# When the gate is normalized: six of its eight iterations in the first half expert, two in the second, and the second matrices' preparation in the blocks between

## The chip, the core and the metric

The kernel runs on one core of a Trainium2 chip. The core has five engines with a queue each, in program order: TensorE (PE, matrix products), VectorE (DVE), ScalarE (ACT), GpSimd (POOL) and SyncE (SP, which here issues the DMAs). An instruction waits on semaphores for results of other engines; whatever stands behind it in its queue waits with it. The metric is the device time of one execution in microseconds; lower is better.

## The reference

Three stages, all in float32. An attention over 2 x 8 heads of 576 positions with a position bias; a layer of three products and a maximum (512 to 768 to 512); and a mixture of 8 experts over 1152 tokens, in which this change lies:

```
logits = x @ w_gate;  P = exp(logits - logits.max())
for _ in range(8):
    P /= P.sum(1, keepdims=True) + 1e-09      # per token: "rows"
    P /= P.sum(0, keepdims=True) + 1e-09      # per expert: "cols"
    P *= N / E
for e in range(E):
    out += P[:, e:e + 1] * (np.maximum(x @ w1[e], 0.0) @ w2[e])
```

P is 1152 x 8. The eight iterations are one chain: each needs the one before it whole.

## The kernel before

Float32 products are made of three float16 products, of a high and a low part of each operand (`h` and `l` at a name's end), scaled by powers of two that are read off the largest magnitudes.

The mixture runs as 32 blocks and 16 half experts. Block n, `up(n)`, makes a quarter of an expert's hidden layer for all tokens by Strassen's scheme: seven products of 12 matmuls each (L1229) into three PSUM banks x, z, y, in the order x, z, y, x, y, x, z. The first, third, fourth and sixth product are copied out by ACT as snapshots s1, s5, s2, s3 (L1237); the second, fifth and seventh are joined to a snapshot by DVE (L1241), and the sum of s3 and s5 is made at L1281. A bank may be started anew only when its reader has read it: the fifth product (y) waits for snapshot s5, the next block's first product (x) for s3, the next block's second product (z) for the seventh's join. ACT then makes relu's high part (L1245), DVE its low part (L1250). After the segments of a block, 0 to 6, `then` runs what is scheduled there.

Half expert h, `down(h)`, multiplies the hidden layers of blocks 2h and 2h + 1 by 512 rows of w2, in nine parts t = 0 to 8 of 12 matmuls with 512 columns (L1309), into two PSUM banks in turn; ACT (h = 0, L1314) or DVE (L1320, L1325) adds a part to `acc`. The order is block 0, 1, 2, half expert 0, block 3, 4, half expert 1, block 5, 6, and so on.

Work for what comes later is put into these by hand, as lists by segment (`between`, `extra`) or part (`todo`), and by `sched` into the sixteen steps of the layer before:

- `prep_f(n)`: the weights of block n; six steps: scaling on ACT (L948), four differences and sums on DVE (L952 to L957), high parts on ACT (L960, L964), low parts as differences on POOL (L961, L967).
- `prep_2(i)`, in lists `p2(i)`: a fourth of half expert i // 4's matrix: two ACT instructions (L1040, L1041), a difference on POOL (L1042), and a read of a later matrix on SP.
- `pk(h, kind, i)`: a largest magnitude of a weight tile, on DVE (L810); `peak_join` reduces them (L836), `peak_send` and `peak_get` pass them through DRAM to all partitions, `peak_all` reduces what landed (L807) and makes the powers of two (L783 to L853).
- `rows()`: four DVE instructions on P (L1158 to L1161). `cols(bank)`: a product with ones on PE (`pc`, L1165; the column sum), then four DVE instructions (L1166 to L1169). In `bank` ps_u it takes the z bank, in ps_d one of the two of the half experts.
- `x_steps(1)`, in lists `end(name)`: sums of the blocks' input (t1, t2, tb, t4, DVE L982), their high parts (h2 to h6, ACT L976) and low parts (l2 to l6, L972, DVE or POOL). `m_top` (L1181) and `m_spread` (L1186) bring the largest input to all partitions.

Before, the iterations are spread thus: rows in part 0 of half expert 0, cols and rows in its parts 2, 4, 6, 8, in block 3's segment 4 and block 4's segments 1 and 5, and the last cols in part 2 of half expert 1.

## Time and profile before

| | us |
|---|---|
| median of 3 runs | 1091.41 (1090.27 to 1092.1) |
| profiled execution, time | 1092.23 |
| its span, first to last instruction | 1090.4 |
| PE busy | 1047.3 |
| DVE busy | 800.1 |
| ACT busy | 589.0 |
| POOL busy | 408.4 |

The profile is one execution. An instruction's row has its start and duration from the span's start; idle time in front of it stands in brackets, with what ended it. Instructions overlap a little at their ends, so the next one can start before a row's end. The stretch that the change touches runs from about 364 us (the last steps of the layer before) to 481 us (the end of half expert 1); blocks 5 to 31 and the other half experts keep their order.

### The profile page before, as it was taken

To read this page: it belongs to the slowest core of one execution; us is meant where nothing else is said; L and a number is where in the kernel's file an instruction comes from. 1 tells how busy PE (TensorE), PEld (TensorE's weight loads), DVE (VectorE), ACT (ScalarE), POOL (GpSimd) and SP (SyncE) were. 2 spreads that over 40 slices of the span, in tenths; PEclk is the share of its full clock that TensorE was granted. 3 is DMA by queue.
4 is the path that set the end of the run, shared out by engine and by line. 5 is a ranking of instruction groups with operands and counts; after the bars stand their busy time and mean duration, and the time that the engine had idled before them with its cause. 6 is when DMAs were issued, how large, how long until landed. Compare 5 with 4: busy or idle time off the path is not lost.

```text
span 1090.4 us, 18491 instructions
## 1 busy us (share of the span) xinstructions
PE 1047.3 (96%) x7163; PEld 734.1 (67%) x7163; DVE 800.1 (73%) x1560; ACT 589.0 (54%) x1003; POOL 408.4 (37%) x285
## 2 busy tenths in 40 slices
PE   6779999999999999999999999999999999999998
PEld 3259988999899765655756657566466575665753
DVE  7999999778786878767677566676776666767633
ACT  7989988534334675444544536445445364454530
POOL 6996998122222424053231312412223124132220
PEclk8999999999999999999999999999999999999999
DMA  5888764233324013020221212302212113010002
GB/s 185 270 238 262 238 186 122 69 102 114 95 61 156 20 42 83 20 63 22 62 63 40 63 35 52 81 20 64 60 43 64 35 50 76 26 44 6 1 1 87
DMA packets 40757, 90.48 MB, mean 83 GB/s; under 512 B 8095, under 2 KB 11102, under 8 KB 39774
## 3 DMA queue, kind: packets, MB, share of 16 engines
q1 hardware_dynamic: 40526, 89.01, 28.1%
q8 instruction: 56, 0.92, 0.4%
q10 hardware_dynamic: 144, 0.29, 0.1%
q14 instruction: 31, 0.25, 0.1%
HBM read 75.20 MB, written 13.30 MB: 81 GB/s over the span
## 4 chain that ended last, share of the span: by engine, by line
PE 68%; DVE 19%; ACT 5%; DMA 4%; issue 3%; POOL 2%; DVEq 0%; SPq 0%; ACTq 0%; POOLq 0%
PE d L1309 29%; PE x L1229 11%; PE y L1229 8%; PE z L1229 7%; PE sc L479 2%; PE pv L617 2%; PE o L1080 2%; PE pt L565 2%; DVE ww L115 1%; DVE ww L120 1%; DVE ww L118 1%; POOL s L353 1%; DVE ng L496 1%; PE p L378 1%; DMA all<-peaks 1%
## 5 line engine op out<-in xcount | busy, mean ns | idle before, releaser
L1309 PE MATMUL d<-w2h,hh 128*128 128x512 f16 x576 | 218.3, 379 | 1.8 <-DVE acc L1320 1.6
L1309 PE MATMUL d<-w2h,hl 128*128 128x512 f16 x576 | 218.3, 379 | 0.2 <-DVE hl L1250 0.2
L1309 PE MATMUL d<-w2l,hh 128*128 128x512 f16 x576 | 218.3, 379 | 0.0
L1229 PEld LDWEIGHTS <-w1h 128*128 128x128 f16 x1792 | 175.5, 98 | 53.1 <-issue 5.7
L1309 PEld LDWEIGHTS <-hh 128*128 128x128 f16 x1152 | 112.6, 98 | 134.6 <-issue 3.4
L961 POOL TENSOR_TENSOR w1l<-wf,w1h 128x768 f16<-128x768 f32 x32 | 55.7, 1741 | 304.8 <-ACT w1h L960 271.4
L1245 ACT ACTIVATE hh<-s 128x576 f16<-128x576 f32 x128 | 87.3, 683 | 129.5 <-DVE s L1241 102.5
L1250 DVE SCALAR_TENSOR_TENSOR hl<-s,hh 128x576 f16<-128x576 f32 x128 | 112.6, 881 | 48.1 <-ACT hh L1245 45.6
L1325 DVE SCALAR_TENSOR_TENSOR acc<-d,kh,acc 128x512 f32<-128x512 f32 x126 | 94.0, 746 | 67.0 <-PE d L1309 65.4
L1042 POOL TENSOR_TENSOR w2l<-w2r,w2h 128x512 f16<-128x512 f32 x64 | 77.4, 1221 | 120.1 <-ACT w2h L1041 120.1
L1229 PEld LDWEIGHTS <-w1l 128*128 128x128 f16 x896 | 87.9, 98 | 23.0 <-issue 0.6
L1309 PEld LDWEIGHTS <-hl 128*128 128x128 f16 x576 | 56.4, 98 | 68.5 <-DVE hl L1250 0.7
L967 POOL TENSOR_TENSOR w1l<-wf,w1h 128x1024 f16<-128x1024 f32 x32 | 69.3, 2164 | 76.1 <-ACT w1h L964 76.1
L948 ACT ACTIVATE wf<-wr,pw 128x1024 f32<-128x1024 f32 x32 | 36.5, 1141 | 96.9 <-DVE pm L783 89.3
L1237 ACT ACTIVATE s<-x,cx 128x576 f32<-128x576 f32 x96 | 70.2, 732 | 27.5 <-PE x L1229 27.2
L1241 DVE SCALAR_TENSOR_TENSOR s<-z,cx,s 128x576 f32<-128x576 f32 x64 | 52.3, 818 | 42.7 <-ACT s L1237 31.1
L1229 PE MATMUL x<-xth,w1h 128*128 128x288 f16 x384 | 78.7, 287 | 0.7 <-ACT s L1237 0.7
L1229 PE MATMUL x<-xtl,w1h 128*128 128x288 f16 x384 | 78.8, 287 | 0.4 <-DVE xtl L972 0.4
L964 ACT ACTIVATE w1h<-wf 128x1024 f16<-128x1024 f32 x32 | 33.6, 1049 | 83.2 <-DVE wf L957 83.1
L1229 PE MATMUL x<-xth,w1l 128*128 128x288 f16 x384 | 78.4, 286 | 0.0
L668 PE MATMUL m<-xh,wl 128*128 128x384 f32 x216 | 73.5, 340 | 2.6 <-POOL wl L123 2.6
L668 PE MATMUL m<-xh,wh 128*128 128x384 f32 x216 | 73.7, 341 | 2.0 <-DVE t L899 1.9
(229 smaller groups left out, 2364.3 us busy)
## 6 DMA issues: line engine op xcount, KB each, us to landing
wr<-in_moe_w SPq DMA_DIRECT2D x50, 512.0 KB, 3.7
w2r<-in_moe_w SPq DMA_DIRECT2D x64, 256.0 KB, 2.6
bias_f<-bo SPq DMA_DIRECT2D x36, 295.5 KB, 3.5
bias<-bias_f SPq DMA_DIRECT2D x32, 288.0 KB, 2.9
qk<-in_qk SPq DMA_DIRECT2D x7, 1152.0 KB, 7.2
wr<-in_moe_w_out SPq DMA_DIRECT2D x6, 512.0 KB, 3.5
vr<-in_v SPq DMA_DIRECT2D x8, 320.0 KB, 5.8
bias<-bias_f SPq DMA_DIRECT2D x16, 144.0 KB, 4.8
```

The lines of the kernel that those rows point to most:

```text
L668: T.matmul(out=p[:, :TG], lhsT=ws[:, 128 * c:128 * c + 128], rhs=xs[:, c, TG * g:TG * g + TG], start=(c == 0 and n == 0), stop=(c == 3 and ...
L948: A.activation(out=t[:, 0:4], in_=w1r.pop(n), func=AF.Identity, scale=w_pow[n // 2, 1][:, 2:3])
L961: G.tensor_tensor(out=lo[:, 0:3], in0=t[:, 1:4], in1=hi[:, 0:3], op=ALU.subtract)
L967: G.tensor_tensor(out=lo[:, 3:7], in0=t[:, 4:8], in1=hi[:, 3:7], op=ALU.subtract)
L1042: G.tensor_tensor(out=lo, in0=r, in1=hi, op=ALU.subtract)
L1229: T.matmul(out=ps[bank][:, s, :SH], lhsT=ws[:, i, c, :], rhs=xs[:, j, c, s * SH:s * SH + SH], start=(start and k == 0), stop=(k == 5), **kw)
L1237: A.activation(out=t, in_=src, func=AF.Identity, scale=c)
L1241: V.scalar_tensor_tensor(out=out, in0=z, scalar=scale, in1=out, op0=ALU.mult, op1=ALU.add)
L1245: A.activation(out=o, in_=src, func=AF.Relu)
L1250: V.scalar_tensor_tensor(out=l, in0=src, scalar=0.0, in1=o, op0=ALU.max, op1=ALU.subtract)
L1309: T.matmul(out=pd, lhsT=hs[:, fh, 128 * t:128 * t + 128], rhs=ws, start=(k == 0), stop=(k == 11))
L1325: V.scalar_tensor_tensor(out=acc[:, t, :], in0=pd, scalar=kh[:, 1 + t:2 + t], in1=acc[:, t, :], op0=ALU.mult, op1=ALU.add)
```

## The change

No instruction is added or taken away; the order changes on every engine.

- Normalization: cols and rows now stand in parts 1, 2, 4, 5, 7 and 8 of half expert 0 (after the rows of part 0), in part 3 of half expert 1, and the last cols in its part 6. Blocks 3 and 4 have none.
- Half expert 0 keeps of its other work only the weights of blocks 3 and 4, in other parts than before. Preparation of half expert 1's matrix (p2(4) to p2(7)) goes to segments 1 and 4 of blocks 3 and 4; the maxima of expert 1's second matrix for half expert 2 (pk(2, 2, i)) to block 3's segments 3 to 6, their exchange to block 4. The maxima of the first one, pk(2, 1, i), go to steps 13 and 14 of the layer before, with a wider exchange.
- p2(1) goes from step 14 into block 0's segment 5; the sum tb and its parts h5 and l5 from step 15 into block 0.

```diff
--- before.py
+++ after.py
@@ -871,7 +871,8 @@
                         load_f(n)
                     S10 = ("a",), [(0, 1)]
                     SB = ("b",), [(1, 1), (0, 2)]
-                    SC = ("c",), [(1, 2)]
+                    SC = ("c",), [(1, 2), (2, 1)]
+                    SD = ("d",), [(2, 2)]
                     jk.append(acc.rearrange("p t d -> p (t d)")[:, 0:1024])
 
                     def size_w(i):
@@ -1067,8 +1068,8 @@
                          6: [bs0[0], pk(0, 2, 2), pk(0, 2, 3), lambda: peak_join(*SB)], 7: [b_top, bs0[1], pf1[0]],
                          8: [b_all] + xs_("t1", "tb", "h2", "l2"), 9: xs_("h3", "h5", "t2") + pf1[1:3], 10: xs_("l3", "l5", "h4") + pf1[3:4],
                          11: xs_("l4", "t4") + pf1[4:6] + [pk(1, 2, 0)], 12: xs_("h6", "g6") + [bs1[0], pk(1, 2, 1), pk(1, 2, 2)],
-                         13: [bs1[1], p2(0), pk(1, 2, 3), lambda: peak_join(*SC)], 14: [p2(1), lambda: peak_send(SC[0])],
-                         15: [lambda: last.update(x_steps(1))] + [end(n) for n in ("t1", "t2", "tb", "h3", "h4", "h5", "h2", "l2")]}
+                         13: [bs1[1], p2(0), pk(1, 2, 3), pk(2, 1, 0)], 14: [pk(2, 1, 1), lambda: peak_join(*SC)],
+                         15: [lambda: last.update(x_steps(1))] + [end(n) for n in ("t1", "t2", "h3", "h4", "h2", "l2")]}
                 evs = []
                 for n, g in enumerate((0, 2, 1, 3)):
                     for d in range(4):
@@ -1190,8 +1191,8 @@
                     V.tensor_scalar(out=nc_, in0=c, scalar1=-1.0, scalar2=None, op0=ALU.mult)
                     V.tensor_scalar(out=kx, in0=cx[:, 1:2], scalar1=xs[:, 1:2], scalar2=2.0 ** 8, op0=ALU.mult, op1=ALU.mult)
 
-                between = {(0, 0): [m_top, end("l3")], (0, 1): [m_spread, end("l4"), end("l5")], (0, 2): [end("t4")],
-                           (0, 3): [end("h6"), end("l6")], (0, 6): [p2(2)], (1, 5): [p2(3)],
+                between = {(0, 0): [m_top, end("l3")], (0, 1): [m_spread, end("l4"), end("tb")], (0, 2): [end("h5"), end("t4"), end("l5")],
+                           (0, 3): [end("h6"), end("l6")], (0, 4): [lambda: peak_send(SC[0])], (0, 5): [p2(1)], (0, 6): [p2(2)], (1, 5): [p2(3)],
                            (1, 6): [logits], (2, 1): [flip], (2, 2): [gate], (1, 2): [lambda: peak_get(SC[0])],
                            (2, 0): [lambda: peak_all(*SC)], (2, 6): []}
                 kh_t = {}
@@ -1299,6 +1300,9 @@
                             2: [fa[2], pk(h + 2, 2, 2), pk(h + 2, 2, 3), lambda: peak_join(*S2), lambda: peak_send(S2[0])],
                             3: [fa[3], lambda: peak_get(S2[0])], 4: [fa[4], fa[5]], 5: [p2(0), lambda: peak_all(*S2)],
                             6: [fb[0], fb[1], p2(1)], 7: [fb[2], fb[3], p2(2)], 8: [p2(3), fb[4], fb[5]]}
+                    if h == 0:
+                        todo = {0: [fa[0]], 1: [fa[1], fa[2]], 2: [fa[3]], 3: [fa[4], fa[5]], 4: [], 5: [fb[0]], 6: [fb[1], fb[2]],
+                                7: [fb[3]], 8: [fb[4], fb[5]]}
                     for t in range(NTT):
                         pd = ps_d.tile([128, 512], F32, tag="d", name="d")
                         k = 0
@@ -1312,15 +1316,17 @@
                         if h == 0:
 
                             A.activation(out=acc[:, t, :], in_=pd, func=AF.Identity, scale=kh[:, 0:1])
-                            if t in (2, 4, 6, 8):
+                            if t in (1, 2, 4, 5, 7, 8):
                                 cols(ps_u)
-                            if t in (0, 2, 4, 6, 8):
+                            if t in (0, 1, 2, 4, 5, 7, 8):
                                 rows()
                         elif h == 1:
                             V.scalar_tensor_tensor(out=acc[:, t, :], in0=pd, scalar=kh[:, 0:1], in1=acc[:, t, :],
                                                    op0=ALU.mult, op1=ALU.add)
-                            if t == 2:
+                            if t in (3, 6):
                                 cols(ps_u)
+                            if t == 3:
+                                rows()
                         else:
                             V.scalar_tensor_tensor(out=acc[:, t, :], in0=pd, scalar=kh[:, 1 + t:2 + t], in1=acc[:, t, :],
                                                    op0=ALU.mult, op1=ALU.add)
@@ -1334,8 +1340,11 @@
                         extra = {}
                         if n == 1:
                             extra = {i: [f] for i, f in enumerate(prep_f(2))}
-                        for seg in {3: (4,), 4: (1, 5)}.get(n, ()):
-                            extra.setdefault(seg, []).extend((lambda: cols(ps_d), rows))
+                        if n == 3:
+                            extra = {1: [p2(4)], 3: [pk(2, 2, 0)], 4: [pk(2, 2, 1), p2(5)],
+                                     5: [pk(2, 2, 2)], 6: [pk(2, 2, 3), lambda: peak_join(*SD), lambda: peak_send(SD[0])]}
+                        if n == 4:
+                            extra = {1: [p2(6)], 2: [lambda: peak_get(SD[0])], 4: [p2(7)], 6: [lambda: peak_all(*SD)]}
                         if n == 5:
                             for t in range(NTT):
                                 extra.setdefault(t % 7, []).append(
```

The first place is ACT's queue around block 3. The names are those above; `s<-x` is a snapshot of bank x. Before, from the last weights of block 4 on:

```order
L964 ACTIVATE w1h<-wf 128x1024
L1237 ACTIVATE s_5941<-x,cx 128x576
L1245 ACTIVATE hh<-s_5941 128x576
L1237 ACTIVATE s_5971<-y,cx 128x576
L1237 ACTIVATE s_5986<-x,cx 128x576
L1245 ACTIVATE hh<-s_5986 128x576
L1237 ACTIVATE s_6024<-x,cx 128x576
```

And now (lines are numbered by the changed kernel, one or four higher):

```order
L965 ACTIVATE w1h<-wf 128x1024
L1238 ACTIVATE s_5916<-x,cx 128x576
L1246 ACTIVATE hh<-s_5916 128x576
L1041 ACTIVATE w2r<-w2r,pw 128x512
L1042 ACTIVATE w2h<-w2r 128x512
L1238 ACTIVATE s_5953<-y,cx 128x576
L1238 ACTIVATE s_5968<-x,cx 128x576
L1246 ACTIVATE hh<-s_5968 128x576
L1041 ACTIVATE w2r<-w2r,pw 128x512
L1042 ACTIVATE w2h<-w2r 128x512
L1238 ACTIVATE s_6005<-x,cx 128x576
```

A pair of preparation 4 now stands in front of snapshot s5, one of preparation 5 in front of s3; block 4 has the same two places.

The second place is DVE's queue in block 3, from the fifth product's join to the seventh's. Before, with a normalization:

```order
L1241 SCALAR_TENSOR_TENSOR s_5986<-y,cx,s_5986 128x576
L1166 TENSOR_REDUCE col<-pc 128x8
L1167 TENSOR_SCALAR col<-col 128x8
L1168 RECIPROCAL col<-col 128x8
L1169 SCALAR_TENSOR_TENSOR P<-P,col 128x72
L1158 TENSOR_REDUCE row<-P 128x9
L1159 TENSOR_SCALAR row<-row 128x9
L1160 RECIPROCAL row<-row 128x9
L1161 TENSOR_TENSOR P<-P,row 128x72
L1250 SCALAR_TENSOR_TENSOR hl<-s_5986,hh 128x576
L1281 TENSOR_TENSOR s_5971<-s_6024,s_5971 128x576
L1241 SCALAR_TENSOR_TENSOR s_6024<-z,cx,s_6024 128x576
```

And now, with maxima:

```order
L1242 SCALAR_TENSOR_TENSOR s_5968<-y,cx,s_5968 128x576
L810 TENSOR_REDUCE pk<-w2r 128x1
L1251 SCALAR_TENSOR_TENSOR hl<-s_5968,hh 128x576
L1282 TENSOR_TENSOR s_5953<-s_6005,s_5953 128x576
L810 TENSOR_REDUCE pk<-w2r 128x1
L1242 SCALAR_TENSOR_TENSOR s_6005<-z,cx,s_6005 128x576
```

The normalization's eight instructions are gone from here; a maximum now stands between the sum of two snapshots and the seventh product's join.

The third place is DVE's queue where the layer before ends and block 0 begins; `xm` is a largest magnitude of the input, `t` a sum of it, `nm` the reduction that `m_top`'s transpose feeds. Before:

```order
L810 TENSOR_REDUCE pk<-w2r 128x1
L836 TENSOR_REDUCE pj<-pk 128x1
L810 TENSOR_REDUCE xm<-acc 128x1 x2
L1094 TENSOR_REDUCE m_3624<-xm 128x1
L982 TENSOR_TENSOR t<-acc 128x576
L982 TENSOR_TENSOR t<-acc,t 128x576
L982 TENSOR_TENSOR t<-acc 128x576
L1182 TENSOR_REDUCE nm_5241<-pmx 1x1
```

And now:

```order
L810 TENSOR_REDUCE pk<-w2r 128x1
L810 TENSOR_REDUCE pk<-wr_4839 128x1
L810 TENSOR_REDUCE xm<-acc 128x1
L810 TENSOR_REDUCE pk<-wr_4973 128x1
L836 TENSOR_REDUCE pj<-pk 128x1 x2
L810 TENSOR_REDUCE xm<-acc 128x1
L1095 TENSOR_REDUCE m_3624<-xm 128x1
L983 TENSOR_TENSOR t<-acc 128x576
L983 TENSOR_TENSOR t<-acc,t 128x576
L1183 TENSOR_REDUCE nm_5234<-pmx 1x1
```

Two maxima over 1024 columns moved in front of the last two `xm`; the third `t` moved behind `nm`.

## Rows read from the trace of the kernel before

**Rows 1.** Page, part 1: busy us, share of the span, instructions, by engine.
```profile
PE 1047.3 (96%) x7163; PEld 734.1 (67%) x7163; DVE 800.1 (73%) x1560; ACT 589.0 (54%) x1003; POOL 408.4 (37%) x285
```

**Rows 2.** Windows: length; busy (x) of PE, PEld, DVE, ACT, POOL; clock; DMA.
```profile
405.25:429.27 24.02, 24.02 (x117) 11.66 (x117) 19.05 (x56) 14.11 (x21) 6.12 (x4) 1.00 0.22 55
429.27:444.65 15.38, 12.45 (x88) 9.33 (x88) 11.37 (x23) 8.02 (x13) 6.46 (x5) 0.89 0.20 61
444.65:455.41 10.76, 10.76 (x91) 8.61 (x89) 8.36 (x19) 5.50 (x8) 0.00 (x0) 1.00 0.01 2
455.41:480.80 25.39, 23.83 (x113) 10.83 (x111) 19.41 (x49) 9.19 (x12) 6.07 (x4) 1.00 0.22 52
438.50:442.20 3.70, 3.70 (x18) 2.59 (x18) 0.95 (x3) 0.57 (x2) 0.00 (x0) 0.54 0.00 0
```

**Rows 3.** Timeline of PE: start, us, line, tile; idle time before and releaser.
```profile
418.39 0.34 PE L1165 MATMUL pc<-P,ones 128*128 128x72 f32 x2
...
431.71 0.28 PE L1229 MATMUL z<-xth,w1h 128*128 128x288 f16 x1 [0.81 <-DVE col L1166]
...
438.40 0.28 PE L1229 MATMUL y<-xth,w1h 128*128 128x288 f16 x1 [2.12 <-ACT s L1237]
...
478.19 0.38 PE L1309 MATMUL d<-w2h,hh 128*128 128x512 f16 x1 [0.77 <-DVE acc L1320]
```

**Rows 4.** Timeline of DVE: normalization, last difference of block 3, preparation, landed maxima.
```profile
418.76 0.23 DVE L1166 TENSOR_REDUCE col<-pc 128x8 f32<-128x72 f32 x1 [1.24 <-PE pc L1165]
...
420.48 2.03 DVE L1161 TENSOR_TENSOR P<-P,row 128x72 f32<-128x72 f32 x1
...
444.50 0.75 DVE L1281 TENSOR_TENSOR s<-s,s 128x576 f32<-128x576 f32 x1
445.37 0.82 DVE L1241 SCALAR_TENSOR_TENSOR s<-z,cx,s 128x576 f32<-128x576 f32 x1
...
468.50 0.28 DVE L836 TENSOR_REDUCE pj<-pk 128x1 f32<-128x2 f32 x2
...
476.05 0.42 DVE L807 TENSOR_REDUCE pm<-all 128x2 f32<-128x256 f32 x1 [3.03 <-DMA all<-peaks]
```

**Rows 5.** Timeline of POOL in the first half expert.
```profile
417.55 1.64 POOL L961 TENSOR_TENSOR w1l<-wf,w1h 128x768 f16<-128x768 f32 x1 [20.74 <-issue]
420.30 2.12 POOL L967 TENSOR_TENSOR w1l<-wf,w1h 128x1024 f16<-128x1024 f32 x1 [1.11 <-ACT w1h L964]
```

**Rows 6.** Timeline of ACT in the first half expert.
```profile
416.00 0.69 ACT L1314 ACTIVATE acc<-d,kh 128x512 f32<-128x512 f32 x1 [2.08 <-PE d L1309]
...
418.59 0.69 ACT L1314 ACTIVATE acc<-d,kh 128x512 f32<-128x512 f32 x1 [1.17 <-PE d L1309]
```

**Rows 7.** Timeline of ACT in block 1.
```profile
384.45 1.14 ACT L948 ACTIVATE wf<-wr,pw 128x1024 f32<-128x1024 f32 x1
...
391.60 0.71 ACT L1040 ACTIVATE w2r<-w2r,pw 128x512 f32<-128x512 f32 x1
392.35 0.63 ACT L1041 ACTIVATE w2h<-w2r 128x512 f16<-128x512 f32 x1
```

**Rows 8.** Timeline of PE in block 1: the fifth product.
```profile
386.84 0.41 PE L1229 MATMUL y<-xth,w1h 128*128 128x288 f16 x2 [0.29 <-ACT s L1237]
```

**Rows 9.** Timeline of DVE, then of PE, in block 0.
```profile
369.96 0.75 DVE L982 TENSOR_TENSOR t<-acc 128x576 f32<-128x576 f32 x1
...
370.95 0.38 PE L1186 MATMUL pmx<-nm,ones 1*128 1x1 f32 x2 [1.06 <-DVE nm L1182]
```

**Rows 10.** Chain that ended last, block 4: start, us, what.
```profile
447.87 0.17 PE pc L1165 x2
...
449.52 1.47 PE x L1229 x12
```

**Rows 11.** Groups of DVE, 405 to 481 us: busy, mean ns of one, idle.
```profile
L810 DVE TENSOR_REDUCE pk<-w2r 128x1 f32<-128x512 f32 x8 | 5.1, 677 | 0.0
L810 DVE TENSOR_REDUCE pk<-wr 128x1 f32<-128x1024 f32 x4 | 4.7, 1208 | 0.0
```

## The prediction

> **What bounds the kernel now.** I read the page's busy times first, then the chain of waits, then windows over the blocks that the change touches, then each engine's timeline there. TensorE (PE) is busy 96% of the span [rows 1], and the chain runs through it, so a move counts only where PE has to wait, or stops waiting. Both kernels issue the same products and the same other instructions; only their order differs. So the whole question is which PE stalls go and which come.
>
> The windows [rows 2] show them. The first half expert takes 24.02 us and PE is busy all through. Block 4 takes 10.76 with PE never idle, column sums included. Block 3, with the same seven products, takes 15.38. A column sum costs PE 0.17, a product 1.47 [rows 10]; block 3 has one sum where block 4 has two, so it should take 10.59 and loses 4.8. The second half expert takes 25.39; by the first, with three sums fewer, it should take 23.5: it loses 1.9. That is 6.7 us in all, the most that any order of this stretch can win.
>
> What PE waited for is in rows 3: VectorE (DVE) still held the column sum's bank (0.81); the fifth product of block 3 waited 2.12 for a snapshot of ScalarE (ACT) that stood behind a join that stood behind the normalization on DVE; and the last part of the second half expert waited 0.77 for an accumulation that stood behind the landed maxima. After the 2.12 the granted clock is 0.54 over 3.70 us, with PE busy all the time: 3.70 x 0.46 = 1.7 us of the 4.8 belong to that.
>
> [...]
>
> **The change part by part.** Times below count from the start of the half expert or product named.
>
> *The first half expert.* One part lasts (24.02 - 4 x 0.17) / 9 = 2.59. A normalization starts when the sum has landed, and its last instruction starts 1.72 later (418.76 to 420.48 [rows 4]) and takes 0.23 like the reduction before it; with 0.37 from the sum's issue to its landing (418.39 to 418.76 [rows 3, 4]) the next sum is possible 2.3 after the last. Sums in neighbouring parts are 2.59 + 0.17 = 2.76 apart, so bare normalizations fit, with 0.46 to spare. What doesn't fit is GpSimd (POOL). In row 420.48 the 72-column multiplication takes 2.03 instead of 0.23: it ends with POOL's difference of 420.30, 2.12 long [rows 4, 5]. So I let DVE instructions with two operands in SBUF wait for a POOL difference that runs. [...]
>
> The two differences start 1.55 and 1.71 after the accumulation of their part [rows 5, 6]. Part 7 (parts are counted from 0) issues the first difference of block 4's weights. Its accumulation comes 0.20 after the part's end (418.59 against 418.39), so the difference runs from 1.75 to 3.39; the sum of part 7 is issued at 0, so the last multiplication would start at 0.37 + 1.72 = 2.09, is held until 3.4, ends at 3.65, and the sum of part 8, wanted at 2.76, waits 0.9. The same sum for part 3's difference (1.91 to 4.03) against part 4's sum holds one of its instructions for 0.4 to 0.85, against 0.46 to spare: 0 to 0.45, I take 0.2. The wait of 0.81 [rows 3] goes, since nothing but the normalization is then before the bank's reading. Bounds of these two: 0 to 1.4; taken 1.1.
>
> *Block 3, fifth product.* After the sum of part 8 the normalization meets the last difference of block 4's preparation (2.12) in the same way: it ends some 1.0 later than the join could start. That is what is left of the long wait. New in front of the fifth product is preparation 4: ACT does two instructions, 391.60 to 392.98 together, 1.28 until the next can start [rows 7], between the relu and the snapshot that the fifth product needs. Block 1 shows such a case: one instruction of 1.14 (row 384.45) in the same place, and the fifth product waited 0.29, start to start 0.45 [rows 7, 8]; 1.28 instead of 1.04 (the pitch of that one) makes it 0.7. I take 0.75 for such a pair. The fifth product so waits 1.0 + 0.75 = 1.75 where it waited 2.12 (2.29 start to start) and then ran at half clock. Bounds: 0.7 (no lateness of the join) to 2.3.
>
> *Blocks 3 and 4, the other preparations.* Preparation 5 stands before the snapshot of the sixth product, on which block 4's first product waits: 0.75. The late snapshot also feeds the sum of two snapshots (row 444.50), which has two operands in SBUF like 420.48 and meets preparation 5's difference on POOL: that starts with the snapshot, lasts about 1.1 (512 of the 768 columns of 417.55, an estimate) and so holds the sum some 0.35 past the snapshot (about 0.7, as 391.60). Then come a maximum of 0.68 that stands there now [rows 11] and the join (row 445.37) that frees the bank: 0.35 + 0.75 + 0.68 + 0.82 = 2.6 after the snapshot, with which block 4's first product started; its second is wanted 1.47 later: 1.1 (0.8 if POOL doesn't hold it). In block 4 two relus, two differences, a maximum and a join follow on DVE, by the same durations about 0.35 later than the product: with preparation 6 in front of the fifth product's snapshot 0.75 + 0.35 = 1.1. Preparation 7's snapshot holds no bank that the half expert wants, but delays DVE. Together 2.95, none of it there before. Lower bound 0, if ACT (busy 5.50 of the 10.76 of block 4 [rows 2]) takes the pairs in its gaps; upper 3.9.
>
> *Second half expert.* Block 4's DVE work ends late and the maxima of expert 1's second matrices are unpacked there (about 0.75): the first accumulation ends 0.55 after the third part wants its bank, and two maxima of 1.21 behind it [rows 11] cost the fourth part another 0.35. The landing of the next maxima comes 7.55 after the last local reduction, and the last part starts 2.14 after that [rows 3, 4]; that reduction comes some 2 us after where it stood in the half expert, but the parts themselves are 0.9 and two sums later: 0.85 instead of 0.93. The accumulation that stood behind maxima and a normalization (part 5) is clear, since the normalization now follows it. Together 1.75 instead of 1.9; bounds 0.8 to 3.0.
>
> *Before the first half expert.* The wait of 1.06 before row 370.95 goes almost whole: the difference of row 369.96 (0.67 until the next) no longer stands before it, nor does one preparation's POOL work [rows 9]. That is -1.1. In front of the last maximum over the input stand two maxima of 1.21 [rows 11], mostly in DVE's idle time: +0.2; preparation 1 in block 0: +0.1. The peaks that block 2 unpacks are two instead of one, four small instructions and a wider reduction, some 0.6 (476.05 to 478.19 holds two items and an accumulation); they stand before a join on which a snapshot and with it the fifth product of block 2 hang: +0.6, or 0 if there is room. Net -0.2; bounds -1.3 to +0.8.
>
> The exchange of maxima over DRAM of the four moved ones has block 4 to land: no cost. The queue on SP gets one read of 64 KB and one of 128 KB where it had them the other way round; nothing waits there.
>
> Sum: 1.1 + 1.75 + 2.95 + 1.75 = 7.55 us of stalls instead of 6.7, and -0.2 before: +0.65. The profiled execution took 1092.23 (span 1090.4, 1.8 around it) and would take 1092.9; the median 1091.41 lies 0.8 lower, so the forecast for the median is 1092.1. All lower bounds together would give 1.5 - 6.7 - 1.3 = -6.5, all upper ones 10.6 - 6.7 + 0.8 = +4.7; the terms hang on two causes (ACT's pairs, POOL's differences), so the rivals below take them by cause.
>
> **Rivals.** (A) ACT takes the moved pairs in its gaps: then the 2.95 and 0.75 of block 3 go, +0.65 - 3.7 = -3.05, 1088.4. For it speaks that ACT is idle for half of block 4, and the pair of 391.60, after which PE doesn't wait; against it, that this pair stands behind the last snapshot of its block while the four moved ones stand in front of one, and [rows 7, 8].
>
> (B) Half clock comes again. The new stalls stand close together: 1.75, 0.75 and 1.1 within some 9 us, and 1.1 again behind them. If the clock falls once more for the 3.70 of rows 2, that costs 1.7: +2.35, 1093.8; twice, 1095.5. It decides from the point where block 3's wait reaches about the 2.12 that did it before. Against it: no single new one is as long, and the two shorter ones of the second half expert (0.77 the last) left its window at 1.00 [rows 2, 3]. [...]
>
> (C) POOL's differences and the normalizations miss each other: 1.1, the 1.0 of block 3 and 0.3 of block 4 go, +0.65 - 2.4 = -1.75, 1089.7. For it: the meeting in part 7 is decided by 0.3 us. Against it: row 420.48 met with less.
>
> **How the numbers follow.** Forecast 0.48, A 0.14, B 0.24, C 0.14. This kernel can tell about 0.2%, 2.2 us, from no change. Faster than 1089.2: A, 0.14. Slower than 1093.6: B, 0.24 (its first case is just beyond, its second well). Same: the forecast and C, 0.62. The range reaches into A and over both cases of B: 1088.9 to 1095.4; the forecast's own is 1090.4 to 1093.4.
>
> **What would show it.** Windows, each up to the next one's first product: block 3 7 x 1.47 + 1.75 + 0.75 = 12.8 instead of 15.38, block 4 10.3 + 1.1 + 1.1 = 12.5 instead of 10.76; the fifth products of both waiting on a snapshot, block 4's second product on a join; a sum of part 8 waiting about 0.9 with the multiplication before it over 1 us long; the row of 370.95 without its wait; the clock 1.00 in all of these windows. I am wrong if block 4 stays below 11.5 (then A), or if the clock is low in blocks 3 and 4 (then B).

## The result and the profile after

The changed kernel takes 1096.47 us (median of six runs, 1095.65 to 1097.51), the kernel before 1090.84 beside it (six runs, 1089.91 to 1092.19): ratio 1.0051, 95% interval 1.0038 to 1.0064. That is slower, outside the range of 1088.9 to 1095.4. Timed once more beside the kernel before (below) the ratio was 1.0042 [1.0028, 1.0056].

The profiled execution took 1095.99 (span 1094.2) against 1092.23. The windows of the changed stretch, first product to first product, in the order first half expert, block 3, block 4, second half expert (start:end, length, then busy time and count of PE, PEld, DVE, ACT, POOL, the clock, DMA):

```profile
406.58:432.30 25.72, 24.84 (x122) 11.99 (x121) 17.31 (x56) 12.55 (x18) 5.40 (x3) 1.00 0.14 41
432.30:444.94 12.64, 10.61 (x86) 8.20 (x86) 7.83 (x15) 7.21 (x11) 3.88 (x3) 1.00 0.08 22
444.94:457.56 12.62, 10.61 (x84) 8.19 (x84) 8.09 (x13) 6.96 (x11) 1.72 (x2) 1.00 0.42 30
457.56:484.57 27.01, 24.14 (x114) 11.06 (x112) 22.66 (x54) 10.49 (x15) 7.76 (x6) 1.00 0.27 72
```

Against [rows 2] block 3 gains 2.7, and everything beside it loses: 1.7, 1.9 and 1.6. The half clock is gone: the granted clock is 1.00 in all four windows, where block 3 had 0.89. Together 77.99 where it was 75.55. The path from block 0 to the first half expert loses as well: from the transposition of the input's maximum (pmx) to that half expert's first product 37.96 us instead of 37.09.

These are PE's waits in the timeline after that are new or longer than before (start, us, line, tile, idle time before and what ended it); they answer to [rows 3], the first one to [rows 9]:

```profile
370.29 0.38 PE L1187 MATMUL pmx<-nm,ones 1*128 1x1 f32 x2
...
376.87 0.41 PE L1230 MATMUL x<-xth,w1h 128*128 128x288 f16 x2 [0.83 <-ACT s L1238]
...
380.98 0.41 PE L1230 MATMUL x<-xth,w1h 128*128 128x288 f16 x2 [0.81 <-ACT s L1238]
...
401.66 0.41 PE L1230 MATMUL y<-xth,w1h 128*128 128x288 f16 x2 [0.70 <-ACT s L1238]
...
423.00 0.41 PE L1166 MATMUL pc<-P,ones 128*128 128x72 f32 x2 [0.19 <-DVE P L1162]
...
432.05 0.41 PE L1166 MATMUL pc<-P,ones 128*128 128x72 f32 x2 [0.69 <-DVE P L1162]
...
439.70 0.41 PE L1230 MATMUL y<-xth,w1h 128*128 128x288 f16 x2 [1.36 <-ACT s L1238]
...
444.94 0.41 PE L1230 MATMUL x<-xth,w1h 128*128 128x288 f16 x2 [0.67 <-ACT s L1238]
...
447.49 0.41 PE L1230 MATMUL z<-xth,w1h 128*128 128x288 f16 x2 [0.91 <-DVE s L1242]
...
453.15 0.40 PE L1230 MATMUL y<-xth,w1h 128*128 128x288 f16 x2 [1.10 <-ACT s L1238]
...
464.26 0.38 PE L1313 MATMUL d<-w2h,hh 128*128 128x512 f16 x1 [1.36 <-DVE acc L1324]
...
476.63 0.38 PE L1313 MATMUL d<-w2h,hh 128*128 128x512 f16 x1 [1.35 <-DVE acc L1324]
```

The wait before pmx's second matmul is gone (the first row has no bracket). In its place stands one in block 0's sixth product (376.87); block 1's first product (380.98) and block 2's fifth (401.66) wait longer than before. Then come the sums of parts 5 and 8, three waits on ScalarE's snapshots, one on a join, and two on accumulations in the second half expert. In the text a wait is counted start to start, about 0.16 more than the bracket: 1.0; 0.97 (before 0.69) and 0.87 (before 0.29); 0.35, 0.86; 1.53, 0.83, 1.08, 1.26; 1.52 and 1.52 (and 0.32 in part 3 there).

What made PE wait stands in the timelines of the other engines. ScalarE, first the snapshot that block 0's sixth product wants, then block 3 (hh is the relu, w2r and w2h are preparation 4, s the snapshot that the fifth product wants):

```profile
376.08 0.74 ACT L1238 ACTIVATE s<-x,cx 128x576 f32<-128x576 f32 x1 [1.44 <-PE y L1230]
...
437.07 0.68 ACT L1246 ACTIVATE hh<-s 128x576 f16<-128x576 f32 x1 [2.36 <-DVE s L1242]
437.66 0.71 ACT L1041 ACTIVATE w2r<-w2r,pw 128x512 f32<-128x512 f32 x1
438.39 0.63 ACT L1042 ACTIVATE w2h<-w2r 128x512 f16<-128x512 f32 x1
438.93 0.72 ACT L1238 ACTIVATE s<-y,cx 128x576 f32<-128x576 f32 x1
```

In block 3 1.27 us of the pair lie between relu and snapshot; before the relu ScalarE was idle for 2.36. DVE, in the order block 0, first half expert, start of the second, its part 3:

```profile
375.24 0.75 DVE L973 TENSOR_TENSOR xtl<-t,xth 128x576 f16<-128x576 f32 x1
...
420.53 0.83 DVE L1168 TENSOR_SCALAR col<-col 128x8 f32<-128x8 f32 x1
...
430.50 1.40 DVE L1162 TENSOR_TENSOR P<-P,row 128x72 f32<-128x72 f32 x1
...
433.21 2.10 DVE L1170 SCALAR_TENSOR_TENSOR P<-P,col 128x72 f32<-128x72 f32 x1
...
462.70 0.28 DVE L807 TENSOR_REDUCE pm<-all 128x1 f32<-128x128 f32 x1 [0.71 <-DMA all<-peaksd]
...
463.47 0.74 DVE L1324 SCALAR_TENSOR_TENSOR acc<-d,kh,acc 128x512 f32<-128x512 f32 x1
...
472.64 1.11 DVE L1168 TENSOR_SCALAR col<-col 128x8 f32<-128x8 f32 x1
...
474.02 0.91 DVE L1170 SCALAR_TENSOR_TENSOR P<-P,col 128x72 f32<-128x72 f32 x1
...
475.83 1.40 DVE L1324 SCALAR_TENSOR_TENSOR acc<-d,kh,acc 128x512 f32<-128x512 f32 x2
```

and POOL's differences beside them:

```profile
419.20 2.13 POOL L968 TENSOR_TENSOR w1l<-wf,w1h 128x1024 f16<-128x1024 f32 x1 [1.28 <-ACT w1h L965]
...
430.18 1.64 POOL L962 TENSOR_TENSOR w1l<-wf,w1h 128x768 f16<-128x768 f32 x1 [8.85 <-issue]
433.10 2.12 POOL L968 TENSOR_TENSOR w1l<-wf,w1h 128x1024 f16<-128x1024 f32 x1 [1.29 <-ACT w1h L965]
...
471.59 2.13 POOL L968 TENSOR_TENSOR w1l<-wf,w1h 128x1024 f16<-128x1024 f32 x1 [6.70 <-ACT w1h L965]
473.69 1.15 POOL L1043 TENSOR_TENSOR w2l<-w2r,w2h 128x512 f16<-128x512 f32 x1
```

Read the two fences together. Each long row of the normalization ends with a POOL row: 421.36 and 421.33, 431.90 and 431.82, 435.31 and 435.22, 473.75 and 473.72, 474.93 and 474.84. The accumulation of 463.47 stands behind a maximum that landed at 462.70, and that of 475.83 behind the whole normalization of part 3. (Its 1.40 are two accumulations.)

The way of that maximum over DRAM stands in SyncE's timeline, first after, then before (the exchange of [rows 4]):

```profile
449.76 0.33 SPq L63 DMA_DIRECT2D peaksd<-pj  x1
...
457.56 0.33 SPq L63 DMA_DIRECT2D all<-peaksd  x1
```
```profile
468.80 0.33 SPq L63 DMA_DIRECT2D peaks<-pj  x1
472.44 0.33 SPq L63 DMA_DIRECT2D all<-peaks  x1
```

From the write's issue to the read's there are 7.8 us where it had been 3.6; the wait that ends last in front of the read is the one for the write (3.4). VectorE then stood idle for 0.71 (row 462.70).

### The profile page after: what moved, and what is told of

It is laid out like the page before. It is cut to its first block, busy times and chain, and to the rows that moved or that the text cites. A ratio compares the mean times of both kernels' runs of the same rounds, so it can differ in the third digit from the quotient of the medians.

```text
span 1094.2 us, 18494 instructions
## 1 busy us (share of the span) xinstructions
PE 1044.5 (95%) x7163; PEld 730.7 (67%) x7163; DVE 799.7 (73%) x1560; ACT 589.0 (54%) x1003; POOL 408.0 (37%) x285
## 4 chain that ended last, share of the span: by engine, by line
PE 65%; DVE 21%; ACT 6%; DMA 4%; issue 3%; POOL 1%; DVEq 0%; ACTq 0%; SPq 0%; POOLq 0%
PE d L1313 28%; PE x L1230 11%; PE y L1230 8%; PE z L1230 7%; PE o L1081 2%; PE sc L479 2%; PE pv L617 2%; DVE pk L810 2%; PE pt L565 2%; DVE ww L115 1%; DVE ww L120 1%; DVE ng L496 1%; DVE ww L118 1%; DVE bo L397 1%; PE p L378 1%
```

## The experiments

One table first, since nearly every verdict rests on it: lengths from PE's timeline, first product to first product; "head" runs from the transposition of the input's maximum to the first half expert, "rest" holds blocks 5 and 6. The execution as a whole varies by some us ahead of this stretch (that transposition lies at 367.3 to 372.2), so the stretch tells more than one run's time. It is not free of scatter either: two more profiles of the kernel before gave sums of 133.67 and 136.83 (e10, e11), one more of the changed kernel 136.67 (e12).

| kernel | head | half expert 0 | block 3 | block 4 | half expert 1 | rest | sum |
|---|---|---|---|---|---|---|---|
| before | 37.09 | 24.02 | 15.38 | 10.75 | 25.37 | 20.66 | 133.27 |
| changed | 37.96 | 25.72 | 12.64 | 12.62 | 27.01 | 20.65 | 136.60 |
| e1 buffers exchanged | 36.55 | 25.73 | 12.64 | 12.61 | 27.25 | 20.71 | 135.49 |
| e2 preparations moved | 37.95 | 25.72 | 11.53 | 10.53 | 28.30 | 20.84 | 134.87 |
| e3 normalizations only | 37.09 | 29.65 | 11.96 | 10.29 | 23.90 | 20.91 | 133.80 |
| e4 preparations, maxima only | 37.48 | 24.02 | 12.59 | 13.60 | 28.01 | 20.65 | 136.35 |
| e5 maximum read later | 37.97 | 25.73 | 12.64 | 12.61 | 25.09 | 20.75 | 134.79 |
| e6 split in part 6 | 37.97 | 26.21 | 11.95 | 12.61 | 27.16 | 20.58 | 136.48 |
| e7 normalization in block 4 | 37.96 | 25.72 | 12.64 | 15.82 | 25.47 | 20.74 | 138.35 |
| e8 all | 35.68 | 26.21 | 10.29 | 13.11 | 23.48 | 20.69 | 129.46 |
| e9 all, second step | 35.25 | 24.79 | 10.29 | 10.46 | 23.48 | 20.73 | 125.00 |

The theory was that four collisions, each of a moved instruction with something that stood there already, make the loss: a shared buffer in block 0, pairs on ScalarE before snapshots, POOL's differences on normalizations, and accumulations behind the landed maximum and the normalization. The rivals stand in the expectations.

**e1: the buffer of tb.** The changed kernel with

```diff
-t1, tb, t2 = (... for q, t in ((sn, "s3"), (sn, "s2"), (w1s, "tx")))
+t1, tb, t2 = (... for q, t in ((sn, "s2"), (sn, "s3"), (w1s, "tx")))
```

> The changed kernel with the buffers of t1 and tb exchanged (tb in the buffer of snapshot s3, t1 in that of s2); no instruction moves. Theory (the 0.995 us before block 0's sixth product is the snapshot s2 waiting for the read of tb, 375.24 to 375.99, out of the buffer that both share): that stall falls under 0.2, and the time by 0.8 to 1.0, to 1095.5 to 1095.7. Rival (the fourth product that the profile names, or ScalarE's own queue, holds the snapshot): the stall stays at 0.9 to 1.0 and the time at 1096.5 +-0.4.

Measured: ratio to before 1.0022 [1.0010, 1.0035], in a comparison of its own (1097.62 against 1094.66, where the kernel before had taken 1090.84 in the first one), so the absolute times of the expectation can't be held against it; the stretch is 1.11 shorter. In the timelines of PE and ACT the sixth product runs on without a bracket, and its snapshot starts while DVE still works on tb's low half (378.81 to 379.55):

```profile
379.20 0.41 PE L1230 MATMUL y<-xth,w1l 128*128 128x288 f16 x2
379.45 0.41 PE L1230 MATMUL x<-xth,w1h 128*128 128x288 f16 x2
```
```profile
377.52 0.68 ACT L977 ACTIVATE xth<-t 128x576 f16<-128x576 f32 x1 [0.94 <-DVE t L983]
378.24 0.74 ACT L1238 ACTIVATE s<-x,cx 128x576 f32<-128x576 f32 x1
```

The stall of 1.0 is the reuse of one buffer; the head gets 1.41 shorter, the rest of it in the products behind. The ACT row of 376.08 above names PE as the releaser of the late snapshot, and PE is not it: what had just ended was DVE's reading of tb (375.24 + 0.75 = 375.99).

**e2: the four preparations elsewhere.** Segment 0 and 3 of a block lie behind a snapshot and before a relu that waits for DVE:

```diff
-extra = {1: [p2(4)], 3: [pk(2, 2, 0)], 4: [pk(2, 2, 1), p2(5)],
+extra = {0: [p2(4)], 3: [p2(5), pk(2, 2, 0)], 4: [pk(2, 2, 1)],
...
-extra = {1: [p2(6)], 2: [lambda: peak_get(SD[0])], 4: [p2(7)], 6:
+extra = {0: [p2(6)], 2: [lambda: peak_get(SD[0])], 3: [p2(7)], 6:
```

> The changed kernel with the four preparations of blocks 3 and 4 on other steps: each pair stands before a relu that waits 2.0 to 2.4 us for VectorE, in place of before a snapshot that frees a bank. Theory (ScalarE's pairs ahead of snapshots are the largest part of the loss): block 3's fifth product 1.53 -> under 0.3, block 4's first 0.83 -> under 0.2, second 1.08 -> under 0.3, fifth 1.26 -> under 0.3, and the load behind preparation 6 leaves earlier, so that part 2 of half expert 1 waits 0.5 to 1.5 in place of 1.52: 3.7 to 5.0 less, 1091.5 to 1092.8. Rival (the stalls are VectorE's, or the half clock comes back where nothing else waits): at most 1.5 less, 1095 or more, or the stretch shows a granted clock near 0.5.

Measured: ratio 1.0019 [1.0005, 1.0033]. Block 4 has no wait over 0.25 left, and block 3's 0.83 on the way to it is gone: 3.2 us, as expected. The stretch as a whole gets 1.73 shorter, not 3.7 to 5.0, since two expectations failed. Block 3's fifth product still waits 1.25, and part 2 of half expert 1 waits 2.81 instead of less. Both stand in DVE's timeline of this run:

```profile
437.15 1.23 DVE L1162 TENSOR_TENSOR P<-P,row 128x72 f32<-128x72 f32 x1
438.30 0.81 DVE L1242 SCALAR_TENSOR_TENSOR s<-z,cx,s 128x576 f32<-128x576 f32 x1
...
461.87 0.28 DVE L807 TENSOR_REDUCE pm<-all 128x1 f32<-128x128 f32 x1 [3.66 <-DMA all<-peaksd]
```

The normalization of part 8 now meets the earlier preparation's POOL difference (437.14, 1.15), so the join comes a microsecond later, and the pair's time is only exchanged for it. The maximum lands 12.98 after its sending (448.89), in the changed kernel 12.94 (449.76 to 462.70): the way over DRAM did not get shorter with the block, so what block 4 won, the accumulation waited. The half clock came back behind the 2.81 (0.50 from 463.4 to 466.4), as the rival had allowed for.

**e3 and e4: the two halves of the change.** e3 is the kernel before with the new places of the normalizations alone; e4 the changed kernel with the normalizations and most of the head of before (the two maxima in steps 13 and 14 and their wider exchange stay moved).

```diff
e3, on the kernel before:
-if t in (2, 4, 6, 8): cols(ps_u)
-if t in (0, 2, 4, 6, 8): rows()
+if t in (1, 2, 4, 5, 7, 8): cols(ps_u)
+if t in (0, 1, 2, 4, 5, 7, 8): rows()
...
-for seg in {3: (4,), 4: (1, 5)}.get(n, ()):
-    extra.setdefault(seg, []).extend((lambda: cols(ps_d), rows))
```

> The kernel before with the changed places of the normalizations alone; preparations, maxima and the head as before. Theory (VectorE of half expert 0 was as full as it can be: six normalizations beside six maxima and two splits): the column sums of several parts wait 1 us or more each, and acc is not delayed there because ScalarE writes it; blocks 3 and 4 lose their stalls (2.29, and the half clock): 1091 to 1096. Rival (the new places are what costs in the changed kernel, not the preparations): 1095 or more with stalls in half expert 1. Rival (the new places are free): 1089 or less.

> The changed kernel with the normalizations and the head of the kernel before: only preparations 4 to 7 and the four maxima are moved to the blocks. Theory (pairs before snapshots cost): stalls of about 1.5, 0.8, 1.1 and 1.3 in blocks 3 and 4 as in the changed kernel, half expert 0 without the 0.97 that it had, the part 2 wait in half expert 1 present: 1093.5 to 1097. Rival (the pairs are covered, and the normalizations' places cost): 1089.5 to 1091.5.

Measured: e3 0.9994 [0.9981, 1.0006], no difference; e4 1.0020 [1.0006, 1.0034]. In e3 the sums of parts 5 and 8 wait 1.50 and 3.47, block 3 has no wait but 1.65 of half clock behind the 3.47 (0.50 from 434.2 to 437.3), block 4 runs without a wait (10.29) and half expert 1 loses its waits: what the blocks win, the first half expert pays, as the theory had it. In e4 every stall of the preparations is there without the new normalizations (1.47, 0.66, 1.89, 1.09, then 2.19). So the normalizations alone are even, and the preparations and maxima alone lose: 0.20% by the ratio, 3.1 in the stretch, about 1.5 of that as a lower clock in half expert 1 (0.94) that the whole change does not have (1.00). The two halves do not add up to the whole, since each meets instructions that the other moves.

**e5: the landed maximum read later.**

```diff
-6: [lambda: peak_all(*SD)]}        # block 4
+if h == 1: todo[4].append(lambda: peak_all(*SD))
```

> The changed kernel with one call moved: the reading of the fourth expert group's maximum (peak_all of SD) from the end of block 4 to part 4 of half expert 1. Theory (part 2 of half expert 1 waits because the first acc of VectorE stands behind a maximum whose way over DRAM, written 449.76 and landed 462.7, is longer than block 4): part 2's wait falls from 1.52 to 0.4 or less, all others stay: 1.1 to 1.5 less. Rival (VectorE's maxima and splits of that half expert make acc late anyhow): part 2 or part 3 waits 1 or more.

One profile: part 2's wait is under 0.25 (part 3 keeps 0.29), and half expert 1 takes 25.09 instead of 27.01. In DVE's timeline the accumulation follows block 4's work at once:

```profile
463.18 1.59 DVE L1251 SCALAR_TENSOR_TENSOR hl<-s,hh 128x576 f16<-128x576 f32 x2
464.69 0.74 DVE L1326 SCALAR_TENSOR_TENSOR acc<-d,kh,acc 128x512 f32<-128x512 f32 x1
```

The theory holds (the stretch is 1.81 shorter), and part 6's wait fell from 1.52 to 0.84 unasked: the DVE queue arrives at part 3 earlier. So 0.7 of part 6's wait had come from the landed maximum too. A wait of 0.31 comes back in the last part.

**e6: POOL's differences away from the last normalizations.**

```diff
-4: [], 5: [fb[0]], 6: [fb[1], fb[2]], 7: [fb[3]], 8: [fb[4], fb[5]]}
+4: [fb[0]], 5: [fb[1], fb[2]], 6: [fb[3], fb[4], fb[5]], 7: [], 8: []}
```

> The changed kernel with GpSimd's three differences of half expert 0 all in its parts without a normalization (the second split's ScalarE and GpSimd steps from parts 7 and 8 to part 6). Theory (GpSimd holds VectorE in the normalizations of parts 5 to 8: 1.40 at 430.50, 2.10 at 433.21): the column sum of part 8 waits 0.86 -> under 0.2, and block 3's fifth product 1.53 -> 0.2 to 0.6, since the join before it is no longer behind the last normalization: 1.6 to 2.2 less. Rival (VectorE is late by its own work, without GpSimd): part 8 keeps 0.5 or more and block 3's fifth product 1.2 or more.

One profile: the stretch is even (136.48). Block 3's fifth product waits 0.83 instead of 1.53, less than before but over the 0.2 to 0.6 expected, and part 8's sum waits 1.35 instead of 0.86, because the longer difference now meets part 7's normalization. DVE, then POOL:

```profile
430.40 1.87 DVE L1170 SCALAR_TENSOR_TENSOR P<-P,col 128x72 f32<-128x72 f32 x1
...
434.57 0.23 DVE L1170 SCALAR_TENSOR_TENSOR P<-P,col 128x72 f32<-128x72 f32 x1
```
```profile
428.46 1.64 POOL L962 TENSOR_TENSOR w1l<-wf,w1h 128x768 f16<-128x768 f32 x1 [6.25 <-issue]
430.06 2.13 POOL L968 TENSOR_TENSOR w1l<-wf,w1h 128x1024 f16<-128x1024 f32 x1
```

The instruction that took 2.10 beside POOL takes 0.23 without it. So POOL holds these instructions, and the rival (VectorE late by its own work) falls as a cause, though part 8 kept its wait; the time taken for part 7 was wrong.

**e7: part 3's normalization behind block 4's first product.**

```diff
-if t in (3, 6): cols(ps_u)
-if t == 3: rows()
+if t == 6: cols(ps_u)
...
+if n == 4: extra[0] = [lambda: cols(ps_d), rows] + extra.get(0, [])
```

> The changed kernel with the normalization of part 3 of half expert 1 put behind block 4's first product. Theory (acc of part 4 stands behind that normalization, which GpSimd holds for 1.6 us more): the 1.52 before part 6 of half expert 1 goes to under 0.2, and block 4's second product does not wait longer than its 1.08, because VectorE is idle between the first and second product: 1.2 to 1.6 less. Rival (acc is late by the maxima of parts 0 to 2): part 6 keeps 0.7 or more, or the second product of block 4 gets over 1.5.

One profile: part 6's wait is gone and block 4's second product waits 0.90, but its fifth 3.07 instead of 1.26, and behind it the granted clock is 0.50 from 456.1 to 458.8. The premise was wrong: DVE is not idle there, it has two relu differences, a maximum and its join first (to 450.63), so the normalization pushed the next join, and with it relu, pair and snapshot. Half expert 1 wins 1.5, block 4 loses 3.2, of it 1.8 as that wait and about 1.3 as half clock.

**e8 and e9: all of it.** e8 joins e1, e2, e5, e6 and e7, and reads the third group's maximum in part 3 of half expert 0. e9 mends what e8 showed:

```diff
e9 against e8:
-5: [fb[1], fb[2]], 6: [fb[3], fb[4], fb[5]]
+5: [fb[1], fb[2]], 6: [pk(2, 2, 0), pk(2, 2, 1), fb[3], fb[4]]     # fb[5] in block 3, segment 2
-extra = {0: [p2(4)], 3: [p2(5), pk(2, 2, 0)], 4: [pk(2, 2, 1)], 5: [pk(2, 2, 2)], 6: [pk(2, 2, 3), join, send]}
+extra = {0: [p2(4)], 2: [fb[5]], 3: [p2(5), pk(2, 2, 2)], 4: [pk(2, 2, 3), join], 5: [send]}
-block 4: extra[0] = [cols, rows]
+block 4: extra[2] = [cols, rows]
-(0, 6): [p2(2)], (1, 5): [p2(3)]
+(1, 5): [p2(2)], (2, 0): [p2(3)]
```

> All remedies together: buffers of t1 and tb exchanged, the four preparations on steps where ScalarE waits for VectorE, the second split of half expert 0 in part 6, the fourth group's maximum in part 4 of half expert 1, the third group's in part 3 of half expert 0, and part 3's normalization behind block 4's first product. Theory (the loss of the changed kernel is the sum of these collisions, 1.0 + 0.6 + 0.9 + 1.5 + 0.8 + 1.1 + 1.3 + 1.5 + 1.5 = 10.2): stalls over 0.25 us between the first product of block 0 and the end of half expert 1 add up to 3 to 5 in place of 14.7, and the time is 5 to 10 below that of the changed kernel, 0 to 5 below that of the kernel before on the same chip. Rival (what is taken away at one place returns at the next, or as half clock): less than 4 below the changed kernel's stretch, or a stretch with a granted clock near 0.5.

> All remedies of the run before, and where that still waited: the last difference of block 4's weights on GpSimd behind block 3's second product (it held the normalization of part 7, 1.35 before the sum of part 8), two of the four maxima in part 6 of half expert 0 and two beside block 3's joins (the last stood ahead of block 4's normalization, 2.59 before its fifth product), that normalization behind block 4's third product, and preparations 2 and 3 one place later (0.75 before block 1's first product). Theory (the same three causes): these three waits fall under 0.4 together: 3.0 to 4.3 less than the run before, 7 to 8.5 below the kernel before. Rival (VectorE is full, what is moved only waits elsewhere): less than 1.5 below the run before.

Measured: e8 1090.24 against 1094.29, ratio 0.9965 [0.9954, 0.9977]; e9 1087.20 against 1095.39, ratio 0.9925 [0.9906, 0.9945]. The waits over 0.25 from block 0 to half expert 1 add up to 14.7 in the changed kernel, 7.6 in e8 (3 to 5 expected), 3.2 in e9. e8 kept 1.35 before part 8's sum and 2.59 before block 4's fifth product, both collisions that e6 and e7 had shown; e9 took them away. Windows of e9, same order as above:

```profile
406.07:430.86 24.79, 24.60 (x122) 12.09 (x122) 18.53 (x67) 12.64 (x17) 5.41 (x3) 1.00 0.15 43
430.86:441.16 10.30, 10.30 (x87) 8.23 (x87) 6.50 (x16) 7.27 (x11) 4.94 (x3) 1.00 0.08 27
441.16:451.61 10.45, 10.45 (x88) 8.40 (x86) 8.04 (x19) 7.85 (x12) 2.31 (x2) 1.00 0.52 37
451.61:474.90 23.29, 23.29 (x112) 10.76 (x110) 18.08 (x45) 9.10 (x12) 5.90 (x4) 1.00 0.29 75
```

Block 3 takes seven products of 1.47 and nothing else, block 4 one sum more, half expert 1 no wait at all. The 0.58 of block 2's fifth product went as well in e8, where its maxima are read later. The rival that what is taken away returns elsewhere falls.

**e10, e11 and e12: the two kernels again.** Unchanged, for what the first profiles had left open.

> The kernel before, unchanged, for a second profile of it. Theory (the half clock of 438.5 to 442.2 came in that one execution only, so that the prediction put 1.7 us of it into the time before): the clock is 1.00 from the first product of block 3 to the end of half expert 1, and block 3 takes 13.5 to 13.9 in place of 15.38. Rival (the wait of 2.12 always brings it): block 3 takes 15.2 to 15.6 with a stretch near 0.54.

> The kernel before, unchanged, for a third profile of it, with the same expectations: without the half clock block 3 takes 13.5 to 13.9, with it 15.2 to 15.6; if the second and the third differ, it comes in some executions.

> The changed kernel, unchanged, timed and profiled once more beside the kernel before. The two profiles put 3.5 us of loss into the changed stretch (from the first maximum's transposition to half expert 2's first product 136.60 against 133.27, and 0.2 ahead of it), the two medians 5.6. Theory (the stretch is the whole loss; the other 2 us are executions of before and after that differ where the program does not): 3.0 to 4.2 above the kernel before, and the stretch again 136.2 to 137.0. Rival (the change costs somewhere else too): 5 or more above the kernel before.

Measured: both profiles of before have the half clock behind block 3's fifth product again, so my theory of a single event falls and the prediction rightly counted it. Windows of e10, then of e11:

```profile
441.30:444.40 3.10, 3.10 (x15) 2.21 (x14) 1.91 (x7) 0.68 (x1) 0.00 (x0) 0.50 0.00 0
```
```profile
439.80:443.00 3.20, 3.20 (x16) 2.24 (x15) 0.69 (x1) 0.26 (x1) 0.00 (x0) 0.51 0.00 0
```

Block 3 takes 16.00 and 15.44 there; in e11 half expert 1 takes 28.63, since the landed maxima made its last part wait 2.55. The changed kernel's stretch is the same to 0.1 (e12: 136.67), and its time 1098.04 against 1094.47. That is 3.6 us above by the medians and 4.6 by the ratio, whose interval goes from 3.1 to 6.1: it does not decide between 3.5, the stretch, and 5.6, the first medians, whose own interval goes from 4.1 to 7.0. Against all three profiles of the kernel before the stretch gives less, about 2.0, since e11's landing came late. So the traces locate 2 to 3.5 us, and the rest of the medians' difference is not located. Behind the stretch the profiles take much the same time (589.0 to 591.2 for the kernel before, 589.0 and 589.3 for the changed one), and ahead of it they scatter. One such case is a half clock (0.50) from 206.8 to 209.6 in the first profile of before, which cost 1.4: the first profile of the changed kernel has none there (1.00 from 195 to 220), but the second (e12) again shows 0.93 over those 25 us, as that of before does.

## Why the prediction was wrong

It forecast +0.65 on the profile's own time; the stretch gave +3.3, and 0.2 more came ahead of the transposition. The medians moved by 5.6, of which 2 are not located (e12); what follows is the account of the traces. Step by step:

- *First half expert*: right. Sums of parts 5 and 8 wait 0.35 and 0.86 (0.2 and 0.9 forecast), held by POOL; rows 430.50 and 433.21 and e6 show the cause. In front of part 5's sum, though, it was a TENSOR_SCALAR with one operand (row 420.53) that POOL held, which the prediction had not counted among those that wait. The 0.81 of [rows 3] is gone.
- *Block 3's fifth product*: right in mechanism, 1.53 for 1.75. e2 and e6 show both halves of it, the pair and the held normalization. Block 3 takes 12.64 for the 12.8 forecast.
- *Other preparations*: right, 0.83, 1.08 and 1.26 for 0.75, 1.1 and 1.1; block 4 takes 12.62 for 12.5. e2 takes them away, e4 shows them alone. Rival A (gaps of ScalarE) is false for the places chosen, though not for the neighbouring ones.
- *Before the first half expert*: failed. The 1.1 of the second pmx went as forecast, and block 2's fifth product got 0.58 for 0.6. But "net -0.2" was +0.9, and +1.1 with the later transposition: tb moved into block 0, and its buffer is also that of the snapshot that the sixth product wants. The prediction asked what moved out of pmx's way, not which buffer the moved value keeps occupied, and until when. e1 shows the 1.0, and 0.4 behind it.
- *Exchange of maxima*: failed. "Has block 4 to land: no cost" put no number on the way. It takes 12.9 to 13.0 us in the changed kernel and in e2, block 4 took 12.62, and DVE's first accumulation stands behind it: part 2 waits 1.52 for the 0.55 forecast (for which no working is shown). Of the difference 0.71 is VectorE's wait for the landing. The trace of before would not have warned of it: with its 7.55 from the last reduction to the landing [rows 4] the maximum would have been there near 457, and VectorE came to it at 462.0. What was longer is the time from the write's issue to the read's, 7.8 to 9.4 us in all ten runs with this exchange, 2.6 to 4.2 in the half experts of the kernel before (three profiles); why is open. e5 shows that part 2's wait goes when the maximum is read later.
- *Second half expert, parts 5 and 6*: failed. "Is clear, since the normalization now follows it" cleared the accumulation ahead of the normalization; the next one stands behind it, and POOL holds two of its instructions. Part 6 waits 1.52 for nothing forecast; e7 shows that it goes with the normalization, e5 that 0.7 of it goes with the late maximum. The last part's 0.85, in turn, is gone: the reduction that its maxima wait for came 0.9 later in the half expert, not 2, and the part itself was wanted 2.6 later, since parts 2 and 6 had waited. (By the prediction's own terms, 2 later against 0.9 and two sums, the 0.85 should have read 1.7.) Together 3.36 for 1.75, above the bound of 3.0.
- *Clock*: right, 1.00 in all four windows. Rival B gave the nearest time (1095.5 in its second case, just outside the stated range of up to 1095.4) and is false as a mechanism; that it came near is luck.

The three failed steps are worth 1.3 + 1.0 + 1.5, less the 0.85 that went: 2.95, and 2.9 lie between the forecast (+0.65) and the traces (3.3 + 0.2). They are of one kind: for a moved instruction the prediction asked what it no longer blocks and what holds it, but at three places not what now waits behind it. At the second place the length of the way, too, was more than any row of before showed.

Which instructions POOL holds the prediction took from one row with two operands [rows 4]; that it holds only such ones was the author's estimate, and no run shows it. The trace of the changed kernel shows others: the TENSOR_SCALAR of 472.64 has one small input and took 1.11 beside POOL, that of 420.53 took 0.83, and the same instruction takes 0.17 elsewhere. Why they take longer there no run shows.

## What to carry to other kernels

For each moved instruction write down three things at its new place: who stands behind it on its engine, who wants the buffer that it reads or writes, and how long its data is under way. On ScalarE, whose rows of block 3 above run one behind the other (437.07 to 439.65), a pair of 1.3 us cost nothing in block 4 right behind a snapshot that frees a bank, where the engine waits for another one anyway (e2), and 0.8 to 1.3 us one step later, just before the next snapshot. In block 3 its difference on POOL moved with it and met a normalization, so the fifth product won only 0.28. Of the single moves three shortened the stretch by 1.1 to 1.8 us (e1, e2, e5), one was even (e6), one made it longer (e7); all of them became worth 11.6 together (e9) only when the collisions that they uncovered were moved as well.

## What was not expected of the hardware

A value sent over DRAM and read back took 12.9 to 13.2 us from the write's issue to the instruction that VectorE had been waiting to start (the changed kernel twice, e1, e2, e6), though the sending came at other times; in the half experts of the kernel before the exchanges took 6.9 to 8.9 (three profiles). The difference is mostly in front of the read's issue (7.8 us and more against 4.2 and less), and no run shows why.

The half clock came in each of three profiles behind the 2.3 us wait of the kernel before (0.54 in [rows 2], 0.50 and 0.51 in the windows above), at a cost of 1.5 to 1.7 us, and in none behind the waits of 0.8 to 1.5 that stand 2.5 to 5.7 us apart in blocks 3 and 4 of the changed kernel (clock 1.00). In the stretches with the longer waits of other runs the clock was low as well: with 2.19 in e4 and 2.81 in e2 (0.94 over half expert 1 in both), 3.07 in e7 (0.50 from 456.1 to 458.8), 3.47 in e3 (0.86 over block 3). With the 2.59 of e8 it was not (1.00 over block 4), so length alone does not settle it; why is open.
